# VectorE's order around the Strassen pairs, the quad weights' loads spread over more places, and four token buffers instead of two

## The chip, the cores and the metric

One core of a Trainium2 chip runs the whole program. The metric is the device time of one execution in microseconds, as the median of several runs. The engines named below are TensorE (PE in the profile, its weight loads PEld), VectorE (DVE), ScalarE (ACT), GpSimd (POOL) and SyncE (SP), which issues almost all DMAs and issues them in order.

## What is computed

An attention block (a gated outer-product recurrence over 768 steps, 4 batches, 8 heads, head size 48) gives a 3072 x 384 matrix. Its rows are then sent to one of eight experts each:

```python
logits = x @ w_gate
expert_idx = np.argmax(logits, axis=1)
...
for e in range(E):
    lo, hi = (boundaries[e], boundaries[e + 1])
    ...
    h = np.maximum(x_sorted[lo:hi] @ w1[e], 0.0)
    y_sorted[lo:hi] = h @ w2[e]
y = y_sorted[inv_perm]
return (gate_w[:, None] * y).astype(np.float32)
```

Here `w1[e]` is 384 x 1024 and `w2[e]` is 1024 x 384, all in float32. The change touches only this second part.

## The kernel before

The first part of the program (attention, routing, and a first tile of 128 rows of experts 0 and 1) is a block of its own, whose instructions stand in an order that is written out by hand. It scatters the rows into the DRAM tensor `xs`, one region to an expert. Its last VectorE steps are `turn(rows_of[0])`, which turns the rows of expert 0 round (written `xT`, L320), and the writing out of the early tile of expert 1.

The second block, again with its order written by hand on every engine, goes over the eight experts. Between the two blocks the framework's scheduler may interleave the two lists of an engine; within a block each engine keeps the order of the code. For each expert `e`:

- `weight_sums` makes three sums of pieces of `w2` on VectorE (`wsum`, L1162, 128x768 each).
- `widen` multiplies the rows with `w1` in eight blocks of 128 hidden columns (TensorE, `hps`, L337). ScalarE and VectorE take turns in moving the results out of PSUM through the ReLU (L347, L349) into `hT`. There are four PSUM banks for this. Experts 0 and 1 have 256 rows left here, two blocks to a bank; experts 2 and 3 have 384 rows, experts 4 to 7 have 352, one block to a bank.
- `hidden_sums` makes two sums of pieces of `hT` on VectorE (`hsum`, L1246, and one at L1162).
- `turn` of the next expert's rows (VectorE, `xT`, one buffer; L320, and `dst`, L326).
- Narrowing. The third tile of experts 2 and 3 is a plain product with `w2` (L353). The third tile of experts 4 to 7 holds 96 rows of the expert and 32 rows of another ("riding", L1143, 128x384). The first two tiles together form one Strassen product, `narrow_pair`: seven products of eight matmuls (L1194), with further sums on VectorE between them (`a[0][0]`, `a[0][1]` of `hT`, and `b[0][1]` of `w2t`, all L1162), ScalarE holding parts (`held`, L1205) and VectorE joining them (`joined`, L1209).

Rows beyond an expert's own room are gathered into two "quads" of four groups of 32 rows, each group with the weights of its own expert (`qw`, eight loads of 1.5 MB to a quad, issued on SP by `fetch` at places numbered 2e and 2e+1: `FIRST_AT` for the first weights, `SECOND_AT` for the second). Quad 0 is widened with expert 4 and quad 1 with expert 7 (`widen_quad`, L1117); `turn_quad` then turns the result with sixteen small VectorE transposes (`hqT`, L1137), four to a group. Quad 0's groups ride with experts 4 to 7, one each; quad 1 is narrowed at the very end (`narrow_quad`, L1143, 128x192).

SP loads, within expert `e`, the rows of expert e+2 (`xrow`, L290, four DMAs), their token numbers and gates (`tg`, L305, two buffers), the first weights of e+2 (L400), the pieces of `fetch(2e)`, the second weights of e+2 (L405), and the pieces of `fetch(2e+1)`. The buffers of a `tg` come free when `narrow_pair` two experts earlier has read its gates.

Of the kernel before, what the change touches and what calls it, by code (L numbers as in the profile page):

```python
# [11 lines left out]
F32 = mybir.dt.float32  # L12
# [8 lines left out]
C = 128  # L21
# [11 lines left out]
E, F = 8, 1024  # L33
NF = F // 128

TILES = 3
# [11 lines left out]
WITH = {4: 0, E - 1: 1}  # L48
# [2 lines left out]
FIXED = np.array([SHORT if e in RIDE else TILES * C for e in range(E)])  # L51

ROWS_AT = {2: 0, 9: 1}
FIRST_AT = {h: (q, g) for q, at in ((0, (3, 4, 5, 6)), (1, (10, 11, 12, 13))) for g, h in enumerate(at)}
SECOND_AT = {3: (0, 0), 4: (0, 1), 5: (0, 2), 6: (0, 3), 10: (1, 0), 11: (1, 1), 13: (1, 2)}

BK = 32
DB = DM // (128 // BK)
# [3 lines left out]
EARLY = 2  # L62

TOK, GATE, USED, ROW = DM, DM + 1, DM + 2, DM + 16
# [57 lines left out]
def kernel(  # L122
# [161 lines left out]
    rowp = ctx.enter_context(tc.tile_pool(name="rowp", bufs=2))  # L284
# [12 lines left out]
    def load_rows(row, count=C):  # L297

        rows = xs[ds(row, count)] if not isinstance(row, int) else xs[row : row + count]
        n, whole = -(-count // C), count // C  # L300
        x = rowp.tile([128, TILES * C // BK, DB], F32, name="xrow")[:, 0 : count // BK]
        tg = rowp.tile([128, TILES, USED - TOK], F32, name="tg")[:, 0:n]
        reads = load_blocks(x, rows)
        reads.append(
            nc.sync.dma_start(  # L305
                tg[:, 0:whole], rows[0 : whole * C, TOK:USED].rearrange("(t p) r -> p t r", p=C)
            ).ins
        )
        if n > whole:
            nc.sync.dma_start(tg[0 : count - whole * C, whole], rows[whole * C :, TOK:USED])  # L310
        return {"n": n, "rows": count, "x": x, "tg": tg, "reads": reads}
# [16 lines left out]
    def widen(x, w, bank, blocks):  # L328

        rows = x["rows"]  # L330
        per = 512 // rows
        for b in blocks:
            i, f = divmod(b, per)
            if f == 0:
                x["h"] = bank(i)[:, 0 : per * rows].rearrange("p (f c) -> p f c", f=per)
            for j in range(KD):
                nc.tensor.matmul(  # L337
                    x["h"][:, f],
                    lhsT=w[0][:, j, b * 128 : b * 128 + 128],
                    rhs=x["xT"][:, j],  # L340
                    start=j == 0,
                    stop=j == KD - 1,
                )
            if f == per - 1:
                to = x["hT"][:, b - f : b + 1]
                if i % 2 == 0:
                    nc.scalar.activation(to, x["h"], AF.Relu)  # L347
                else:
                    nc.vector.tensor_scalar(to, x["h"], 0.0, None, op0=OP.max)  # L349
# [725 lines left out]
    with ExitStack() as st:  # L1075
# [21 lines left out]
        def quad_first(q, g):  # L1097
            x = quads[q]
            if g == 0:
                x["first"] = qp.tile([128, 4, KD, F], F32, name="qw1")  # L1100
            quad_weights(x["first"][:, g], q, g, moe_w1, W1)

        def quad_second(q, g):
            quads[q]["second"][g] = w2 = qp.tile([128, NF, DM], F32, name="qw2", bufs=4)
            quad_weights(w2, q, g, moe_w2, W2)

        def pieces():
            return [(g, slice(g * T, g * T + T)) for g in range(4)]
# [19 lines left out]
                    nc.vector.tensor_scalar(hq[:, b], hp[b], 0.0, None, op0=OP.max)  # L1128
            x["hq"] = hq

        def turn_quad(x):

            x["hT"] = qp.tile([128, NF, C], F32, name="hqT", bufs=2)
            hq = x["hq"].rearrange("p b f (j c) -> p j (b f) c", c=T)
            for g, r in pieces():
                for j, to in pieces():
                    nc.vector.transpose(x["hT"][to, :, r], hq[r, j])  # L1137

# [22 lines left out]
        def minus(to, a, b):  # L1161
            nc.vector.tensor_tensor(to, a, b, op=OP.subtract)  # L1162

        def weight_sums(w):

            b = [
                [w[1][:, HB * i : HB * i + HB, HD * j : HD * j + HD] for j in range(2)]
                for i in range(2)
            ]
            t1, t2, t4 = (qp.tile([128, HB, HD], F32, name=f"wsum{i}") for i in (1, 2, 4))  # L1170
            minus(t1, b[0][1], b[0][0])
            minus(t2, b[1][1], t1)
            minus(t4, b[1][0], t2)
            return b, t1, t2, t4
# [5 lines left out]
                for t in range(2)  # L1180
            ]

        def narrow_pair(x, s1, sums):

            b, t1, t2, t4 = sums
            a = hidden_parts(x)
            one, two, both = (psz.tile([128, DM], F32, name="yps") for i in range(3))
            one, two, left, right = one[:, 0:HD], two[:, 0:HD], both[:, 0:HD], both[:, HD:DM]
            ysb = [ep.tile([128, DM], F32, name="ysb") for t in range(2)]
            gate = [x["tg"][:, t, 1:2] for t in range(2)]  # L1190

            def product(to, h, w, start):
                for f in range(HB):
                    nc.tensor.matmul(  # L1194
                        to,
                        lhsT=h[:, f],
                        rhs=w[:, f],
                        start=start and f == 0,
                        stop=f == HB - 1,
                        skip_group_check=True,  # L1200
                    )

            def held(part, t):
                to = qp.tile([128, HD], F32, name="held", bufs=3)
                nc.scalar.mul(to, part, gate[t])  # L1205
                return to

            def joined(t, h, part, other):
                nc.vector.scalar_tensor_tensor(  # L1209
                    ysb[t][:, h * HD : h * HD + HD],  # L1210
                    part,
                    gate[t],
                    other,
                    op0=OP.mult,
                    op1=OP.add,
                )

            def leave(t):
                scatter(out, x["dst"][:, t : t + 1], ysb[t], N - 1, "out")

            minus(b[0][1], b[1][1], b[0][1])
            product(one, a[0][0], b[0][0], True)
            p1 = held(one, 0)
            minus(a[0][0], s1, a[0][0])
            product(left, a[0][1], b[1][0], True)
            minus(a[0][1], a[0][1], a[0][0])
            product(right, a[1][1], t4, True)
            joined(0, 0, left, p1)
            p4 = held(right, 1)
            product(two, s1, t1, True)  # L1230
            p5 = held(two, 1)
            product(one, a[0][0], t2, False)
            u2 = held(one, 0)
            product(two, a[0][1], b[1][1], False)
            joined(0, 1, two, u2)
            leave(0)
            product(one, a[1][0], b[0][1], False)
            joined(1, 0, one, p4)
            joined(1, 1, one, p5)
            leave(1)  # L1240
# [19 lines left out]
        def fetch(half):  # L1260
            if half in ROWS_AT:
                quads[ROWS_AT[half]] = quad_rows(ROWS_AT[half])
            if half in FIRST_AT:
                quad_first(*FIRST_AT[half])
            if half in SECOND_AT:
                quad_second(*SECOND_AT[half])

        for e in range(E):
            x, w = rows_of[e], weights[e]
            end = e == E - 1  # L1270
            x["hT"] = qp.tile([128, NF, TILES * C], F32, name="hT")[:, :, 0 : x["rows"]]
            sums = weight_sums(w)
            widen(x, w, bank, range(NF))
            if e in WITH:
                widen_quad(quads[WITH[e]])
            s1 = hidden_sums(x)
            if e + 1 < E:
                turn(rows_of[e + 1])
            if e + 1 in WITH:
                turn(quads[WITH[e + 1]], qp)  # L1280
            if e + 2 < E:
                rows_of[e + 2] = load_expert(e + 2)
                load_first_weights(e + 2)
            fetch(2 * e)
            if e in WITH and not end:
                turn_quad(quads[WITH[e]])
            if e in RIDE:
                narrow_riding(x, w, quads[0], RIDE[e])
            if end:
                nc.gpsimd.drain()  # L1290
                quad_second(1, 3)
                halves_of(quads[WITH[e]], 0)
                turn_quad(quads[WITH[e]])
            for t in range(2, TILES - 1 if e in RIDE else x["n"]):
                narrow_late(x, t, w)
            narrow_pair(x, s1, sums)
            if end:
                narrow_quad(quads[WITH[e]])
            if e + 2 < E:
                load_second_weights(e + 2)  # L1300
            fetch(2 * e + 1)
# [156 lines left out]
```

## Time and profile before

| | |
|---|---|
| median of 3 runs | 402.71 us (402.61 to 405.11) |
| profiled execution, its own time | 400.64 us |
| its span | 398.6 us |
| mean granted TensorE clock | 0.976 |
| PEld, busy | 293.8 us (74%) |
| ACT, POOL, busy | 115.1 us (29%), 105.2 us (26%) |
| DMA, mean over the span | 238 GB/s |

The span runs from the first to the last instruction of the program on the core; the execution's own time is 2.04 us longer. Busy shares are means over the whole span, so they don't tell which stage waits for what. In a timeline row stand the start, the duration, the engine, the line, what is written and read, and in square brackets the idle time of the engine before it with what ended that. In a row of waits stand the total, the count and the longest.

### The profile page before, as it was taken

What the parts mean: (1) busy time and instruction counts of PE and PEld (TensorE: products, weight loads), DVE (VectorE), ACT (ScalarE), POOL (GpSimd) and SP (SyncE); (2) the same over time, 40 slices, a digit from 0 to 9 for tenths busy, and PEclk for the clock granted to TensorE, in tenths of its full rate; (3) what the DMA queues carried; (4) which work ended last, traced back from release to release, by engine and by line L of the source; (5) the groups of instructions that cost most, each with busy time, mean ns of one, the idle gap of its engine ahead of it and who ended that gap; (6) DMA issues with size and microseconds to landing.
All of it is one profiled execution on the core that took longest, in us unless ns stands there. A gap on an engine that the chain in (4) does not pass through costs nothing.

```text
span 398.6 us, 8241 instructions
## 1 busy us (share of the span) xinstructions
PE 377.1 (95%) x3246; PEld 293.8 (74%) x3246; DVE 223.3 (56%) x447; ACT 115.1 (29%) x222; POOL 105.2 (26%) x120
## 2 busy tenths in 40 slices
PE   8999999999999969999999999977999999999774
PEld 8889989889997849897568568522964965963573
DVE  6999989897856244636254164137344435422740
ACT  6998867784231001111001001100110110201010
POOL 5453357479746010202012012000210210200002
PEclk9999999999999989999999999996999999999969
DMA  8999766759964559492489999890073389990501
GB/s 272 385 363 373 241 238 217 255 173 371 406 204 161 171 150 310 78 349 53 176 280 299 351 394 321 344 339 14 16 248 123 89 304 384 403 400 20 178 10 55
DMA packets 51663, 94.86 MB, mean 238 GB/s; under 512 B 20840, under 2 KB 40875, under 8 KB 49568
## 3 DMA queue, kind: packets, MB, share of 16 engines
q1 hardware_dynamic: 48448, 84.62, 63.3%
q0 software_dynamic: 3168, 9.64, 6.5%
q8 instruction: 27, 0.44, 0.5%
q14 instruction: 20, 0.16, 0.1%
HBM read 79.23 MB, written 15.21 MB: 237 GB/s over the span
## 4 chain that ended last, share of the span: by engine, by line
PE 79%; DMA 8%; DVE 6%; issue 2%; SPq 2%; ACT 1%; POOL 0%; POOLq 0%; DVEq 0%
PE hps L337 26%; PE yps L1194 15%; PE yps L1143 7%; PE s L594 6%; PE xp L717 6%; PE yt L618 6%; DMA w2t<-in_moe_w_dram 4%; PE yps L353 3%; PE yt L639 3%; PE kp L607 3%; PE dp L655 2%; DVE hqT L1137 2%; DMA fpack<-c_fpack 2%; PE hps L1117 1%; PE s L337 1%
## 5 line engine op out<-in xcount | busy, mean ns | idle before, releaser
L337 PE MATMUL hps<-xT,w1t 128*128 128x352 f32 (+2 forms) x384 | 111.8, 452 | 4.0 <-DVE xT L320 3.4
L337 PEld LDWEIGHTS hps<-xT,w1t 128*128 128x128 f32 x384 | 73.9, 193 | 39.4 <-issue 4.0
L196 POOL DMA_INDIRECT out_dram<-ysb,dst x24 | 29.3, 1223 | 232.2 <-DVE ysb L364 144.7
L349 DVE TENSOR_SCALAR hT<-hps 128x352 f32<-128x352 f32 (+2 forms) x28 | 15.6, 558 | 74.0 <-PE hps L337 74.0
L1194 PE MATMUL yps<-w2t,hT 128*128 128x192 f32 x256 | 46.3, 336 | 0.5 <-ACT held L1205 0.5
L1194 PEld LDWEIGHTS yps<-w2t,hT 128*128 128x128 f32 x256 | 43.5, 196 | 4.2 <-issue 2.5
L347 ACT ACTIVATE hT<-hps 128x352 f32<-128x352 f32 (+2 forms) x28 | 13.7, 490 | 111.3 <-PE hps L337 95.8
L1205 ACT ACTIVATE held<-yps,tg 128x192 f32<-128x192 f32 x32 | 12.9, 420 | 103.3 <-PE yps L1194 55.0
L1143 PE MATMUL yps<-qw,hqT 128*32 128x192 f32 (+1 forms) x192 | 29.7, 397 | 4.7 <-DVE hqT L1137 4.7
L600 DVE COPY_PREDICATED at<-mpack,s 128x512 f32<-128x512 uint8 x48 | 32.1, 731 | 3.1 <-PE s L594 3.1
L1209 DVE SCALAR_TENSOR_TENSOR ysb<-yps,tg,held 128x192 f32<-128x192 f32 x32 | 12.6, 415 | 37.1 <-PE yps L1194 37.1
L560 POOL TENSOR_TENSOR k<-k,r 128x1024 f32<-128x1024 f32 (+1 forms) x11 | 25.2, 2294 | 20.5 <-ACT r L556 14.6
L1194 PE MATMUL yps<-wsum,hT 128*128 128x192 f32 x128 | 25.0, 341 | 4.6 <-DVE hT L1162 4.6
L542 DVE TENSOR_TENSOR_SCAN sum<-g,cap 128x1032 f32<-128x1032 f32 (+1 forms) x14 | 28.2, 2019 | 2.0 <-ACT g L535 1.9
L196 POOL DMA_INDIRECT xs<-xr,posi x24 | 25.4, 1060 | 13.5 <-issue 4.6
L594 PE MATMUL s<-q,k 64*128 64x128 f32 x384 | 26.3, 282 | 0.1
L1194 PEld LDWEIGHTS yps<-wsum,hT 128*128 128x128 f32 x128 | 22.2, 199 | 5.2 <-issue 5.1
L717 PE MATMUL xp<-wx,ys 128*128 128x104 f32 x192 | 24.9, 279 | 0.2 <-ACT ys L681 0.2
L594 PEld LDWEIGHTS s<-q,k 64*128 64x128 f32 x384 | 22.8, 188 | 2.6 <-issue 1.2
L1143 PE MATMUL yps<-w2t,hT 128*32 128x384 f32 x192 | 24.5, 539 | 0.0
L618 PE MATMUL yt<-at,v 128*48 128x128 f32 x384 | 24.3, 276 | 0.0
L717 PEld LDWEIGHTS xp<-wx,ys 128*128 128x128 f32 x192 | 22.9, 192 | 1.0 <-ACT ys L681 0.3
(130 smaller groups left out, 497.2 us busy)
## 6 DMA issues: line engine op xcount, KB each, us to landing
qw<-in_moe_w_dram SPq DMA_DIRECT2D x16, 1536.0 KB, 15.0
w1t<-in_moe_w_dram SPq DMA_DIRECT2D x8, 1536.0 KB, 8.2
w2t<-in_moe_w_dram SPq DMA_DIRECT2D x8, 1536.0 KB, 15.7
k<-in_ku_dram SPq DMA_DIRECT2D x12, 512.0 KB, 5.3
q<-in_qu_dram SPq DMA_DIRECT2D x12, 512.0 KB, 6.0
f<-in_fu_dram SPq DMA_DIRECT2D x10, 512.0 KB, 6.0
xs<-pad SPq DMA_DIRECT2D x8, 600.0 KB, 4.6
v<-in_vu_dram SPq DMA_DIRECT2D x12, 384.0 KB, 7.0
```

Of the source, the lines that this page charges most:

```text
L196: ins = nc.gpsimd.indirect_dma_start(out=dst, out_offset=bass.IndirectOffsetOnAxis(ap=idx, axis=0), in_=src, in_offset=None, bounds_check= ...
L337: nc.tensor.matmul(x["h"][:, f], lhsT=w[0][:, j, b * 128 : b * 128 + 128], rhs=x["xT"][:, j], start=j == 0, stop=j == KD - 1,)
L347: nc.scalar.activation(to, x["h"], AF.Relu)
L349: nc.vector.tensor_scalar(to, x["h"], 0.0, None, op0=OP.max)
L542: nc.vector.tensor_tensor_scan(x["sum"][:, part].rearrange("p s c -> p (s c)"), x["g"][:, part].rearrange("p s c -> p (s c)"), cap[:, part ...
L560: ins = on.tensor_tensor(k, k, units[u]["r"][:, part], op=OP.mult).ins
L594: done["score"] = nc.tensor.matmul(ps[h][:, p], lhsT=x["k"][r, s], rhs=x["q"][r, s], start=True, stop=True).ins
L600: nc.vector.copy_predicated(x["at"][:, a, h], _bc(causal, 1, HP), x["ps", a][h])
L618: nc.tensor.matmul(x["yt"][a][DP * (h ^ a) : DP * (h ^ a) + D, p], lhsT=x["v"][:, a, 2 * p + h], rhs=x["at"][:, a, h, p], start=p == 0, st ...
L717: nc.tensor.matmul(x["xp", a][:, p], lhsT=x["ys", a][:, p], rhs=wx[:, p, 0:XW] if a else wx[:, p, E:WX], start=True, stop=True,)
L1143: nc.tensor.matmul(yp[r], lhsT=h[:, f, at : at + T], rhs=w[:, f, cols], start=f == 0, stop=f == NF - 1, skip_group_check=True,)
L1194: nc.tensor.matmul(to, lhsT=h[:, f], rhs=w[:, f], start=start and f == 0, stop=f == HB - 1, skip_group_check=True,)
```

## The change

Five things are moved, and one number is set.

1. `weight_sums` stands behind the first four blocks of `widen` instead of ahead of it.
2. In `narrow_pair` the sum `b[0][1]` moves from the front to behind the two sums of `hT`.
3. The turning of the next expert's rows moves, for experts 0 and 1, into `narrow_pair`, behind the first `joined`. For experts 2 to 6 it stays behind `hidden_sums`.
4. Quad 0 is widened between the sixth and seventh block of expert 4. One group (four transposes) is turned right behind it, the other three behind the pair.
5. Quad 1 is still widened behind expert 7, but `hidden_sums` comes ahead of it. Two of its groups are turned ahead of the riding tile and two inside the pair, where all four were turned between the riding tile and the pair.
6. The quads' first weights are fetched at places 2, 3, 4, 5 and 10, 11, 12, 12 (before: 3 to 6 and 10 to 13), the second weights at 6 to 9 and all three at 13 (before: 3 to 6 and 10, 11, 13). `tg` has four buffers.

```diff
-FIRST_AT = {h: (q, g) for q, at in ((0, (3, 4, 5, 6)), (1, (10, 11, 12, 13))) for g, h in enumerate(at)}
-SECOND_AT = {3: (0, 0), 4: (0, 1), 5: (0, 2), 6: (0, 3), 10: (1, 0), 11: (1, 1), 13: (1, 2)}
+FIRST_AT = {2: [(0, 0)], 3: [(0, 1)], 4: [(0, 2)], 5: [(0, 3)], 10: [(1, 0)], 11: [(1, 1)], 12: [(1, 2), (1, 3)]}
+SECOND_AT = {6: [(0, 0)], 7: [(0, 1)], 8: [(0, 2)], 9: [(0, 3)], 13: [(1, 0), (1, 1), (1, 2)]}
...
-        tg = rowp.tile([128, TILES, USED - TOK], F32, name="tg")[:, 0:n]
+        tg = rowp.tile([128, TILES, USED - TOK], F32, name="tg", bufs=4)[:, 0:n]
...
-        def turn_quad(x):
+        def turn_quad(x, some):
...
-            for g, r in pieces():
+            for g, r in pieces()[some]:
                 for j, to in pieces():
                     nc.vector.transpose(x["hT"][to, :, r], hq[r, j])
...
-        def narrow_pair(x, s1, sums):
+        def narrow_pair(x, s1, sums, between=lambda: None):
...
-            minus(b[0][1], b[1][1], b[0][1])
             product(one, a[0][0], b[0][0], True)
             p1 = held(one, 0)
             minus(a[0][0], s1, a[0][0])
             product(left, a[0][1], b[1][0], True)
             minus(a[0][1], a[0][1], a[0][0])
+            minus(b[0][1], b[1][1], b[0][1])
             product(right, a[1][1], t4, True)
             joined(0, 0, left, p1)
+            between()
...
+            quad = quads[WITH[e]] if e in WITH else None
+
+            def turn_next():
+                if e + 1 < E:
+                    turn(rows_of[e + 1])
+                if e + 1 in WITH:
+                    turn(quads[WITH[e + 1]], qp)
+
+            widen(x, w, bank, range(4))
             sums = weight_sums(w)
-            widen(x, w, bank, range(NF))
-            if e in WITH:
-                widen_quad(quads[WITH[e]])
+            if quad and not end:
+                widen(x, w, bank, range(4, 6))
+                widen_quad(quad)
+                turn_quad(quad, slice(0, 1))
+                widen(x, w, bank, range(6, NF))
+            else:
+                widen(x, w, bank, range(4, NF))
             s1 = hidden_sums(x)
-            if e + 1 < E:
-                turn(rows_of[e + 1])
-            if e + 1 in WITH:
-                turn(quads[WITH[e + 1]], qp)
+            if end:
+                widen_quad(quad)
+                halves_of(quad, 0)
+                turn_quad(quad, slice(0, 2))
+            elif e >= EARLY:
+                turn_next()
...
-            if e in WITH and not end:
-                turn_quad(quads[WITH[e]])
             if e in RIDE:
                 narrow_riding(x, w, quads[0], RIDE[e])
             if end:
                 nc.gpsimd.drain()
                 quad_second(1, 3)
-                halves_of(quads[WITH[e]], 0)
-                turn_quad(quads[WITH[e]])
             for t in range(2, TILES - 1 if e in RIDE else x["n"]):
                 narrow_late(x, t, w)
-            narrow_pair(x, s1, sums)
             if end:
-                narrow_quad(quads[WITH[e]])
+                narrow_pair(x, s1, sums, lambda: turn_quad(quad, slice(2, 4)))
+                narrow_quad(quad)
+            else:
+                narrow_pair(x, s1, sums, turn_next if e < EARLY else lambda: None)
+                if quad:
+                    turn_quad(quad, slice(1, 4))
```

More of the change, by code (lines that the diff above doesn't have):

```diff
@@ L1129, in widen_quad @@
             x["hq"] = hq
-        def turn_quad(x):
-            x["hT"] = qp.tile([128, NF, C], F32, name="hqT", bufs=2)
+        def turn_quad(x, some):
+            if "hT" not in x:
+                x["hT"] = qp.tile([128, NF, C], F32, name="hqT", bufs=2)
             hq = x["hq"].rearrange("p b f (j c) -> p j (b f) c", c=T)
-            for g, r in pieces():
+            for g, r in pieces()[some]:
                 for j, to in pieces():
@@ L1262, in fetch @@
                 quads[ROWS_AT[half]] = quad_rows(ROWS_AT[half])
[L1263 to L1266, printed above, removed]
+            for piece in FIRST_AT.get(half, ()):
+                quad_first(*piece)
+            for piece in SECOND_AT.get(half, ()):
+                quad_second(*piece)
         for e in range(E):
```

## The prediction, written before the changed kernel ran

> **What bounds the kernel now.** I read the page's shares first, then TensorE's own waits, then the chain that ended last, and last the timeline around each wait.
>
> ```profile
> span 398.6 us, 8241 instructions
> ...
> PE 377.1 (95%) x3246; PEld 293.8 (74%) x3246; DVE 223.3 (56%) x447; ACT 115.1 (29%) x222; POOL 105.2 (26%) x120
> ...
> PE yps L1143 <- DVE hqT L1137: 4.7, 1, 4.7
> PE yps L1194 <- DVE hT L1162: 4.6, 2, 4.2
> PE hps L337 <- DVE xT L320: 3.4, 1, 3.4
> PE hps L337 <- ACT hT L347: 0.6, 1, 0.6
> ```
>
> TensorE is the bound: 95% busy. VectorE is at 56% and yet ends all its long waits, three of them, once each. So VectorE isn't short of time. It is late in three places. They show in the timeline:
>
> ```profile
> 134.78 5.41 PE L353 MATMUL yp<-w2t,hT 128*128 128x384 f32 x16
> 136.30 0.14 DVE L1047 CAST fixi<-fix 1x1 int32<-1x1 f32 x1
> 140.38 0.96 DVE L1162 TENSOR_TENSOR wsum<-w2t 128x768 f32<-128x768 f32 x1 [3.94 <-PE yp L353]
> 142.25 1.20 DVE L320 STREAM_TRANSPOSE xT<-xrow 128x768 f32<-128x768 f32 x1
> 143.59 8.62 PE L337 MATMUL hps<-xT,w1t 128*128 128x256 f32 x31 [3.40 <-DVE xT L320]
> ...
> 267.98 1.58 DVE L320 STREAM_TRANSPOSE xT<-xrow 128x1056 f32<-128x1056 f32 x1
> 269.51 7.19 DVE L1137 STREAM_TRANSPOSE hqT<-hq 32x256 f32<-32x256 f32 x16
> 271.34 0.85 PE L1143 MATMUL yps<-qw,hqT 128*32 128x384 f32 x1 [4.72 <-DVE hqT L1137]
> ...
> 371.85 7.17 DVE L1137 STREAM_TRANSPOSE hqT<-hq 32x256 f32<-32x256 f32 x16
> 379.04 0.96 DVE L1162 TENSOR_TENSOR w2t<-w2t 128x768 f32<-128x768 f32 x1
> 380.74 2.90 PE L1194 MATMUL yps<-wsum,hT 128*128 128x192 f32 x8 [4.22 <-DVE hT L1162]
> ```
>
> At 140 the turning of expert 0's rows stands behind two weight sums, which stand behind TensorE's last early tile. At 271 the riding tile waits for the turning of quad 0, behind `xT`. At 381 the Strassen pair waits for its sums, behind sixteen transposes and `b[0][1]`. A gap costs more than its length, as the granted clock (before the DMA share and GB/s at the end of the row) shows:
>
> ```profile
> 140.00:150.00 10.00, 6.59 (x23) 5.35 (x23) 4.46 (x6) 0.60 (x1) 1.44 (x1) 0.83 0.53 156
> 270.00:280.00 10.00, 8.66 (x61) 3.03 (x62) 6.86 (x16) 0.00 (x0) 0.00 (x0) 0.66 0.01 3
> 380.00:390.00 10.00, 9.26 (x84) 8.61 (x88) 2.78 (x6) 1.15 (x3) 1.94 (x2) 0.68 0.07 23
> ```
>
> So I price whole stages by the chain, a disturbed stage against an undisturbed one of the same work:
>
> ```profile
> 143.59 12.30 PE hps L337 x48
> 165.59 10.37 PE hps L337 x48
> 186.19 15.48 PE hps L337 x48
> 206.83 9.10 PE yps L1194 x56
> ...
> 245.67 6.65 PE hps L337 x23
> 288.89 14.20 PE hps L337 x48
> ...
> 308.39 9.30 PE yps L1194 x56
> 317.69 14.20 PE hps L337 x48
> ...
> 346.48 14.20 PE hps L337 x48
> 360.68 5.29 PE hps L1117 x48
> 365.97 5.20 PE yps L1143 x64
> ...
> 387.69 5.38 PE yps L1143 x128
> ```
>
> **The change part by part.** *Weight sums behind four blocks.* In the second block's list VectorE's first instruction is now an eviction of expert 0, which needs `xT`. The sums can't slip ahead of `turn` any more. The turn itself needs its rows:
>
> ```profile
> 131.42 2.18 SPq L290 DMA_DIRECT2D xrow<-xs  x4
> xrow<-xs SPq DMA_DIRECT2D x4, 96.0 KB, 3.0
> ```
>
> They are issued by 133.60 and land 3.0 us later, at 136.6; VectorE is free at 136.44. So `xT` is done at about 137.9, and TensorE goes on at 134.78 + 5.41 = 140.19 without a stop. The stage took 143.59 + 12.30 - 140.19 = 15.70 us. The same 48 matmuls take 10.37 for expert 1. **Gain 5.33.** The sums cost 2.9 us (three of 0.96) behind the evictions of blocks 1 and 3. With 352 rows a block takes 14.20/8 = 1.78: block 3's eviction ends at 7.7 into the stage, the sums at 10.6, and block 5's is due at 10.7. Nothing waits. If the sums were late, three further banks cover some 3.5 us.
>
> *Expert 1's and 2's turns inside the pair, `b[0][1]` later.* The pair of expert 0 took 165.59 - 155.89 = 9.70 us and that of expert 1 186.19 - 175.96 = 10.23, against 9.10 undisturbed. The rows of expert 1:
>
> ```profile
> 181.52 1.54 PE L1194 MATMUL yps<-wsum,hT 128*128 128x192 f32 x8 [0.37 <-DVE hT L1162]
> 183.32 2.87 PE L1194 MATMUL yps<-w2t,hT 128*128 128x192 f32 x16 [0.26 <-ACT held L1205]
> ```
>
> Turn and `b[0][1]` stand ahead of the sum and of the first `joined` that these two wait for; with both out of the way the waits go. **Gain 0.60 + 1.13 = 1.73.** The turn then ends some 6.7 us into the pair, 2.4 ahead of the next `widen`. For experts 2 to 6 `b[0][1]` now delays `joined` by about 0.2 us. ScalarE follows, and TensorE needs its result over a microsecond later: nothing.
>
> *Quad 0 inside expert 4.* From 245.67 to 288.89 the expert took 43.22 us. Expert 5 took 317.69 - 288.89 = 28.80 for the same without a quad, and the quad's matmuls take 5.29 at full clock: 34.09. **Gain 9.13**: the wait of 4.72, the wait of 0.6 for ScalarE's eviction (it stands in this expert, and may return when the banks fall otherwise), and the rest, 3.8, is half clock. Four transposes of 0.45 take 1.8 us while TensorE does two blocks (3.55). The other twelve take 5.4 at the start of expert 5, behind two `joined` of 0.42, so up to 6.2. The first eviction there is due at 3.6 and ends below 7. Its bank is wanted by block 5 at 8.9, so 2 us are left. Beyond that each late microsecond costs one.
>
> *Quad 1 around the last pair.* From 346.48 to 387.69 expert 7 took 41.21 against the same 34.09. **Gain 7.12.** New deadlines, from the start R of the pair:
>
> ```profile
> 312.58 0.42 DVE L1209 SCALAR_TENSOR_TENSOR ysb<-yps,tg,held 128x192 f32<-128x192 f32 x1 [0.66 <-PE yps L1194]
> ...
> 378.00:379.00 1.00, 0.00 (x0) 0.00 (x0) 0.97 (x3) 0.00 (x0) 0.00 (x0) 1.00 0.02 10
> ```
>
> The riding tile starts 5.2 ahead of R, when the quad is done. With 1 us at most for the quad's eviction and two tiny instructions, the first eight transposes run from R - 4.2 to R - 0.6. The first `joined` of expert 6's pair ended at 313.00 with R at 308.39, so at R + 4.6; with `b[0][1]` ahead of it I take R + 4.8. The last eight end at R + 8.4, and `narrow_quad` reads them at R + 9.3: 0.9 us are left. It also reads the last `qw` load, which is issued when the riding tile ends (today at 371.17). In the slice from 378 to 379 the DMAs move almost nothing more (10 GB/s), so it lands by R + 7.8. Today the late pair hides it; then 1.5 us are left. The 5.38 us of `narrow_quad` and the tail behind it stay.
>
> *Loads and four token buffers.*
>
> ```profile
> SPq L305 <- DVE ysb L1209: 59.1, 6, 25.2
> ...
> w2t<-in_moe_w_dram SPq DMA_DIRECT2D x8, 1536.0 KB, 15.7
> ```
>
> SP stood 59.1 us at `tg` until an older pair had read its gates, with the first weights of the next experts queued behind. That goes, but TensorE waits for no DMA in the rows above: gain 0. What is late next on SP are w1's and w2's own buffers, free at the end of `widen` and of the pair; a w2 lands 15.7 us after its issue (median), with a whole expert (28.80) until it is read. Place 2 puts one `qw` ahead of expert 3's w2, and places 7 and 9 put second weights ahead of the rows of experts 6 and 7. Each delays those by its own 1.5 MB, and both are read an expert later. I bound this part by -0.5 and +1.
>
> The sum is 5.33 + 1.73 + 9.13 + 7.12 = 23.31. With half of the 0.6 left standing it is 23.0. The profiled execution (400.64, 398.6 of it span) would fall to 377.6, its span to 375.6. The median of the runs is 2.07 higher, so the forecast is 402.71 - 23.0 = 379.7, 5.7% faster.
>
> [...]
>
> **The rivals.** *Expert 0 starts late all the same* (`xT` waits for something the trace hides behind the sums, or the scheduler puts other work ahead): 5.3 us are not won, 385.0. For it: only the end of a longer wait is seen. Against: rows landed and VectorE idle for 3.94. *The end stalls in a new place:* the last transposes or the last load come after R + 9.3. At 2 to 4 us late with some half clock this gives back 3 to 6: 383 to 386. For it: margins of 0.9 and 1.5 us only. Against: both margins come from rows. *Slower:* TensorE reaches its weights sooner, the loads don't shorten, and a w2 that hasn't landed stops VectorE at `weight_sums` with two evictions behind them, so `widen` stops once four banks are full. It decides from a landing some 11 us into a stage, and to reach 407 it would have to hold TensorE 27 us in all, say 7 in each of experts 2 to 5. Against: the sums stood up to 8 us earlier in the stage before and waited for no DMA. *No effect:* quad and pair wait for other causes; 402 to 403. Against: the releasers are named in the rows.
>
> **How the numbers follow.** The forecast with all four terms has 0.72, expert 0 late 0.10, the end stalled 0.11, no effect 0.04, slower 0.03. The likeliest case spans 377.0 (0.3 and 0.5 from the terms above, and runs some 2 lower, as the profiled one was) to 382. The range goes to 386 and leaves out 2 in 10 at most. About 1% is what a measurement of this kernel can tell from no change. Faster by over 1%: 0.93; within: 0.04; slower: 0.03.
>
> **What would show it.** TensorE's waits for `xT`, `hqT` and `hT` should be gone or below 0.5 us each; the granted clock should be 1.00 in all slices of the second block; expert 0's 48 matmuls should take 10.4 us straight behind the early tile; expert 4 and expert 7 should take 34.1 each up to the end of the pair; SP's wait for `ysb` at L305 should be gone. It would be wrong if a wait of over 3 us on TensorE stands anywhere behind 140 us.

## The result, and the profile after

| | before | after |
|---|---|---|
| median of 4 runs each, taken together | 402.77 us (402.61 to 405.11) | 381.17 us (380.78 to 381.63) |
| profiled execution, its own time | 400.64 us | 381.11 us |
| its span | 398.6 us | 379.1 us |
| mean granted TensorE clock | 0.976 | 0.995 |

The ratio is 0.9451, with an interval from 0.9415 to 0.9487: 5.5% faster. The forecast was 379.7 us. Ratios here and below are taken over the single runs and not from the two medians (381.17/402.77 is 0.946), and they leave out one run of 386.78 us, of the kernel called loads_back below, which lay 1.5% above that kernel's fastest.

The page of the changed kernel, its shares and the granted clock in forty slices (in tenths, 9 is 90% or more):

```profile
span 379.1 us, 8261 instructions
...
PE 369.5 (97%) x3246; PEld 289.5 (76%) x3246; DVE 224.4 (59%) x447; ACT 115.6 (30%) x222; POOL 99.7 (26%) x120
...
PEclk9999999999999999999999999999999999999998
```

The work is the same: TensorE has 3246 matmuls before and after, VectorE 447 instructions. TensorE is busy 7.6 us less (377.1 to 369.5), although it computes the same products. The granted clock accounts for it. In the kernel before it stood at 0.50 in three stretches behind 140 us: 144.11 to 147.52, 270.40 to 277.23 and 379.63 to 386.46. TensorE was busy for 15.0 of these 17.1 us. At the full clock that work is estimated at half the time, so 7.5 us less. In the changed kernel the clock falls only at 375.45, behind the last matmul. The rest of the 19.5 us by which the span is shorter is idle time.

TensorE's waits in the changed kernel (total, count, longest):

```profile
PE yt L754 <- DVE yt L482: 1.6, 1, 1.6
PE yp L353 <- issue: 0.5, 1, 0.5
...
PE yps L1144 <- issue: 0.4, 2, 0.2
```

The first two lie in the first block, which the change leaves alone. The four long or named waits of before (4.7 for `hqT`, 4.6 for `hT`, 3.4 for `xT`, 0.6 for ScalarE's `hT`) are all gone. A new one is in the last line: two stops of 0.18 us for which no other engine is named.

The chain that ended last, in order of time (start, length, engine, line, number of instructions):

```profile
137.13 5.27 PE yp L353 x16
142.40 10.36 PE hps L337 x48
152.76 9.10 PE yps L1195 x56
...
172.22 9.10 PE yps L1195 x56
...
240.80 10.65 PE hps L337 x36
251.45 5.29 PE hps L1117 x48
256.73 3.75 PE hps L337 x12
260.48 5.30 PE yps L1144 x64
265.78 9.30 PE yps L1195 x56
...
332.67 14.20 PE hps L337 x48
...
357.31 9.30 PE yps L1195 x56
366.61 3.42 PE yps L1144 x80
```

From the early tile to the last quad it is TensorE throughout, one stage straight behind the other. Beside before, stage by stage (us):

| stage | before | forecast | after |
|---|---|---|---|
| end of the early tile | 140.19 | 140.19 | 142.40 |
| from there to the end of expert 0's 48 matmuls | 15.70 | 10.37 | 10.36 |
| pair of expert 0, of expert 1 | 9.70, 10.23 | 9.10, 9.10 | 9.10, 9.10 |
| expert 4 to the end of its pair | 43.22 | 34.09 | 34.28 |
| expert 7 to the end of its pair | 41.21 | 34.09 | 33.94 |
| `narrow_quad` | 5.38 | 5.38 | 6.94 |

Each after-value is the difference of two starts in the chain (expert 4: 275.08 - 240.80, where 275.08 = 265.78 + 9.30; `narrow_quad`: 366.61 to 373.55, where VectorE's last eviction is released; TensorE's own rows end at 373.05).

VectorE in the same execution (a timeline row: start, length, engine, line, what is written and read, count, idle time before):

```profile
139.32 1.23 DVE L320 STREAM_TRANSPOSE xT<-xrow 128x768 f32<-128x768 f32 x1 [0.67 <-DMA xrow<-xs]
...
148.38 0.95 DVE L1163 TENSOR_TENSOR wsum<-w2t 128x768 f32<-128x768 f32 x1
...
275.89 5.39 DVE L1138 STREAM_TRANSPOSE hqT<-hq 32x256 f32<-32x256 f32 x12
281.31 0.52 DVE L349 TENSOR_SCALAR hT<-hps 128x352 f32<-128x352 f32 x1
...
353.02 3.58 DVE L1138 STREAM_TRANSPOSE hqT<-hq 32x256 f32<-32x256 f32 x8
...
362.07 3.61 DVE L1138 STREAM_TRANSPOSE hqT<-hq 32x256 f32<-32x256 f32 x8
```

`xT` now starts when its rows land and is done 1.85 us ahead of the end of the early tile (139.32 + 1.23 = 140.55 against 142.40). The first sum runs 6 us into the stage. The twelve transposes of quad 0 hold expert 5's first VectorE eviction until 6.2 us into its stage (281.31 - 275.08), and TensorE doesn't feel it (14.20 us for that stage's 48 matmuls, as for experts 6 and 7). The last eight transposes end at 365.68, 0.86 us ahead of the first matmul of `narrow_quad` that the timeline shows (366.54).

SP's waits that matter:

```profile
SPq L1095 <- PE yps L1144: 28.6, 1, 28.6
SPq L405 <- PE yps L1195: 21.7, 5, 4.9
...
SPq L305 <- ACT held L1206: 1.6, 1, 1.6
```

The 59.1 us at L305 for `ysb` are gone. SP now stands at L405 until an older `w2` has been read (here by TensorE, and 19.4 us more until VectorE's sums have read it), which the prediction named as next; L1095, where it waits for a `qw` buffer, stood at 28.1 us before.

### The profile page after: what moved, and what is told of

Same layout as the page of the kernel before. It is cut to its first block, busy times and chain, and to the rows that moved or that the text cites. A ratio compares the mean times of both kernels' runs of the same rounds, so it can differ in the third digit from the quotient of the medians.

```text
span 379.1 us, 8261 instructions
## 1 busy us (share of the span) xinstructions
PE 369.5 (97%) x3246; PEld 289.5 (76%) x3246; DVE 224.4 (59%) x447; ACT 115.6 (30%) x222; POOL 99.7 (26%) x120
## 4 chain that ended last, share of the span: by engine, by line
PE 93%; DVE 3%; DMA 2%; SPq 1%; issue 0%; POOL 0%; POOLq 0%
PE hps L337 29%; PE yps L1195 19%; PE yps L1144 7%; PE s L594 6%; PE yt L618 6%; PE xp L717 6%; PE s L337 3%; PE hps L1117 3%; PE yps L353 3%; PE kp L607 3%; PE yt L639 2%; PE dp L655 2%; PE yp L353 2%; DMA fpack<-c_fpack 2%; DVE sum L542 1%; SPq L517 1%
## 5 line engine op out<-in xcount | busy, mean ns | idle before, releaser
L337 PE MATMUL hps<-xT,w1t 128*128 128x352 f32 (+2 forms) x384 | 110.1, 446 | 0.0
L337 PEld LDWEIGHTS hps<-xT,w1t 128*128 128x128 f32 x384 | 72.7, 190 | 34.9 <-issue 0.8
L196 POOL DMA_INDIRECT out_dram<-ysb,dst x24 | 23.3, 972 | 215.8 <-DVE ysb L364 134.5
L1195 PE MATMUL yps<-w2t,hT 128*128 128x192 f32 x256 | 44.6, 328 | 0.0
L1195 PEld LDWEIGHTS yps<-w2t,hT 128*128 128x128 f32 x256 | 41.9, 190 | 3.1 <-issue 2.5
L196 POOL DMA_INDIRECT xs<-xr,posi x24 | 27.2, 1135 | 16.2 <-issue 4.9
L1144 PE MATMUL yps<-qw,hqT 128*32 128x192 f32 (+1 forms) x192 | 27.5, 381 | 0.4 <-issue 0.4
L1195 PE MATMUL yps<-wsum,hT 128*128 128x192 f32 x128 | 23.4, 326 | 0.0
L618 PEld LDWEIGHTS yt<-at,v 128*48 128x48 f32 x384 | 20.3, 123 | 2.4 <-issue 1.3
L1144 PE MATMUL yps<-w2t,hT 128*32 128x384 f32 x192 | 21.4, 487 | 0.0
```

Of the source, the lines that this page charges most:

```text
L196: ins = nc.gpsimd.indirect_dma_start(out=dst, out_offset=bass.IndirectOffsetOnAxis(ap=idx, axis=0), in_=src, in_offset=None, bounds_check= ...
L337: nc.tensor.matmul(x["h"][:, f], lhsT=w[0][:, j, b * 128 : b * 128 + 128], rhs=x["xT"][:, j], start=j == 0, stop=j == KD - 1,)
L618: nc.tensor.matmul(x["yt"][a][DP * (h ^ a) : DP * (h ^ a) + D, p], lhsT=x["v"][:, a, 2 * p + h], rhs=x["at"][:, a, h, p], start=p == 0, st ...
L1144: nc.tensor.matmul(yp[r], lhsT=h[:, f, at : at + T], rhs=w[:, f, cols], start=f == 0, stop=f == NF - 1, skip_group_check=True,)
L1195: nc.tensor.matmul(to, lhsT=h[:, f], rhs=w[:, f], start=start and f == 0, stop=f == HB - 1, skip_group_check=True,)
```

## The experiments

Behind L1117 the line numbers of the changed kernel are one or two higher than before's. Executions differ in where the early tile ends, in both kernels, so each part is compared from that end to the end of the span ("second block"). The unchanged changed kernel took 236.73, 236.16 and 235.10 us there in three profiles, the kernel before 258.44 and 256.63. The runs fall into three sessions, on different chips; medians are compared within a session only.

| run | median us | ratio to before, interval | end of early tile | second block |
|---|---|---|---|---|
| after_again | 382.99 | 0.9471 (0.9387 to 0.9555) | 144.85 | 236.16 |
| before_again | 402.52 (one run) | | 143.87 | 256.63 |
| sums_first | 388.88 | 0.9603 (0.9519 to 0.9687) | 145.49 | 242.2 |
| quad0_back | 389.99 | 0.9649 (0.9562 to 0.9736) | 143.37 | 244.3 |
| quad1_back | 384.09 | 0.9596 (0.9556 to 0.9635) | 140.12 | 240.3 |
| quad1_three | 381.18 | 0.9523 (0.9492 to 0.9554) | 140.32 | 238.4 |
| pair_back | 380.22 | 0.9487 (0.9454 to 0.9520) | 141.29 | 236.9 |
| loads_back | 383.35 | 0.9535 (0.9490 to 0.9580) | 141.19 | 240.2 |
| after_third | 378.08 | 0.9452 (0.9409 to 0.9495) | 140.95 | 235.10 |
| tg_back | 377.93 | 0.9462 (0.9403 to 0.9521) | 140.64 | 235.2 |
| places_back | 378.23 | 0.9457 (0.9399 to 0.9514) | 140.83 | 235.3 |
| quad_whole | 377.45 | 0.9450 (0.9394 to 0.9507) | 140.14 | 235.6 |

First session: up to quad0_back, before 403.31. Second: quad1_back to loads_back, before 401.11, without a run of the unchanged new order. Third: the rest, before 399.53.

### Both kernels again

No edit.

> The changed kernel as it is, a second time. Its first profile began the second block 2.2 us later than the profile of before (142.40 against 140.19 us) and took 1.56 us longer for the last quad (6.94 against 5.38). Theory A, both are chance of one execution: this profile begins the block near 140.2 and takes 5.4 for the quad. Theory B, both belong to the changed program: 142.4 and 6.9 again, span 379 us.

> The kernel before, a second time. Its first profiled execution was 2.07 us under the median of its runs. If the slower runs lose that in the first block, the early tile of expert 1 ends here near 142.3 us instead of 140.19, the second block takes the same as before, and the span is near 400.6. If they lose it in the second block, the tile ends near 140.2 and a wait of the second block is longer.

The gain stands: 382.99 against 403.31. Both kernels end the early tile later than in the first profiles (144.85 and 143.87), so that end moves with the execution or the chip and not with the change. The last quad was slow again in after_again (6.46 us) and not in before_again (5.41), so neither theory of the first expectation held as it stood; after_third below has both near their old values. In after_again the late end came from a wait of the early tile itself (TensorE's timeline, then two windows with the columns of the prediction: start and end, length, TensorE's busy time, and the granted clock third from the end):

```profile
126.98 7.12 PE L353 MATMUL yp<-w2t,hT 128*128 128x384 f32 x16 [2.02 <-ACT hT L347]
```

```profile
124.07:127.48 3.41, 1.39 (x10) 1.06 (x10) 0.80 (x5) 0.60 (x1) 1.21 (x3) 1.00 0.31 120
127.48:130.89 3.41, 3.41 (x7) 1.85 (x6) 3.17 (x14) 0.00 (x0) 1.71 (x2) 0.50 0.13 53
```

A wait of 2.02 us was followed by 3.41 us at half clock (0.50), by estimate 1.7 us lost beside the wait. The kernel before shows the opposite case. In before_again its wait for `xT` was again 3.40 us, and the clock stayed full:

```profile
147.27 10.60 PE L337 MATMUL hps<-xT,w1t 128*128 128x256 f32 x48 [3.40 <-DVE xT L320]
```

```profile
142.28:145.69 3.41, 1.59 (x5) 0.58 (x4) 1.59 (x2) 0.00 (x0) 0.00 (x0) 1.00 0.50 115
145.69:149.10 3.41, 1.83 (x9) 1.65 (x10) 2.87 (x5) 0.00 (x0) 1.13 (x1) 1.00 0.05 3
149.10:152.52 3.42, 3.42 (x17) 3.02 (x16) 0.00 (x0) 0.60 (x1) 0.30 (x1) 1.00 0.78 266
```

The 48 matmuls took 10.60 us there (to 157.87) where they took 12.30 in the chain of the first profile. That is nearly all of the 1.81 us between the two second blocks of the kernel before (258.44 and 256.63). The first profile of the kernel before, whose clock did fall, cut the same way:

```profile
140.70:144.11 3.41, 0.52 (x3) 0.49 (x4) 3.38 (x6) 0.00 (x0) 0.00 (x0) 1.00 0.23 48
144.11:147.52 3.41, 3.41 (x10) 2.66 (x9) 0.77 (x1) 0.00 (x0) 1.44 (x1) 0.50 0.44 138
```

The windows here are as long as this stretch at half clock, 3.41 us.

### The weight sums first

```diff
+            sums = weight_sums(w)
             widen(x, w, bank, range(4))
-            sums = weight_sums(w)
```

> The changed kernel with the weight sums ahead of all eight blocks again. Theory of the prediction: two sums of expert 0 slip ahead of the turning of its rows, TensorE waits about 3.4 us for xT and then runs for a window at half clock, together +5.3 us: about 386.5. Rival: the place of the sums inside the stages matters, or the turning waits for its rows anyway: no wait for xT here, within 1 us of the changed kernel.

VectorE's timeline at the boundary of the two blocks:

```profile
145.68 0.96 DVE L1163 TENSOR_TENSOR wsum<-w2t 128x768 f32<-128x768 f32 x1 [3.94 <-PE yp L353]
146.68 0.96 DVE L1163 TENSOR_TENSOR wsum<-w2t,wsum 128x768 f32<-128x768 f32 x1
147.55 1.19 DVE L320 STREAM_TRANSPOSE xT<-xrow 128x768 f32<-128x768 f32 x1
```

The old picture is back: the second block's sums stand ahead of the first block's `xT`, VectorE idles 3.94 us until the early tile is through with TensorE, and TensorE then waits 3.4 us for `xT`. The clock dips after it (0.83 over the 10 us from 148). The chain:

```profile
148.89 12.03 PE hps L337 x48
160.92 9.10 PE yps L1195 x56
```

From the end of the early tile the stage takes 160.92 - 145.49 = 15.43 us, against 10.36: 5.07 more. A wait of 0.58 us for ScalarE's `hT` also comes back, now in expert 3, and with it 0.84 us. The median is 5.9 us above that of after_again (388.88 - 382.99). So the first step holds, with its size.

### Quad 0 behind all blocks again

```diff
-            if quad and not end:
-                widen(x, w, bank, range(4, 6))
+            widen(x, w, bank, range(4, NF))
+            if quad and not end:
                 widen_quad(quad)
-                turn_quad(quad, slice(0, 1))
-                widen(x, w, bank, range(6, NF))
-            else:
-                widen(x, w, bank, range(4, NF))
...
+            if quad and not end:
+                turn_quad(quad, slice(0, 4))
             if e in RIDE:
...
-                if quad:
-                    turn_quad(quad, slice(1, 4))
```

> The changed kernel with quad 0 widened behind expert 4 and all sixteen of its transposes ahead of the riding tile again. Theory: TensorE waits 4 to 5 us for hqT and then runs 5 to 6 us at half clock, +8.5 to +9.1: about 390. Rival: with the loads earlier and the sums elsewhere the transposes start sooner and the wait is under 3 us with no clock lost: +3 at most.

TensorE's waits, and the window behind the wait:

```profile
PE yps L1144 <- DVE hqT L1138: 4.7, 1, 4.7
```

```profile
265.00:275.00 10.00, 8.38 (x59) 2.75 (x60) 6.89 (x17) 0.00 (x0) 0.00 (x0) 0.66 0.07 24
```

Expert 4 takes 42.35 us (241.77 to 284.12 in the chain) against 34.28: 8.07 more, of which 4.7 is the wait and about 3.4 the clock (10 us at 0.66); 8.5 to 9.1 was expected. The median is 7.0 above after_again. In the kernel before the same stretch took 43.22, so 0.87 more: the wait of 0.6 for ScalarE, which the early sums cause and which isn't here, and 0.27 for which no row names a cause (before_again took 43.01, so part of it is chance).

### Quad 1's turning: all of it late, or three quarters of it

quad1_back:

```diff
-            s1 = hidden_sums(x)
             if end:
                 widen_quad(quad)
-                halves_of(quad, 0)
-                turn_quad(quad, slice(0, 2))
+            s1 = hidden_sums(x)
...
                 quad_second(1, 3)
+                halves_of(quad, 0)
+                turn_quad(quad, slice(0, 4))
...
-                narrow_pair(x, s1, sums, lambda: turn_quad(quad, slice(2, 4)))
+                narrow_pair(x, s1, sums)
```

> The changed kernel with quad 1 as before: widened ahead of the hidden sums, all sixteen transposes between the riding tile and the pair. b[0][1] stays late, so the pair's wait for its sums should be 4.2 - 0.9 = 3.3 us, with 1.7 to 3 us of half clock behind it: +5 to +6.5 for the stage from expert 7's start to the end of the pair. The last quad takes 5.4 us if its slower run in the changed kernel (6.4, with a stop 3.6 us in) comes from TensorE arriving without a pause, and 6.4 if that belongs to the quad itself. [...]

quad1_three keeps the order of `hidden_sums` and turns one group early and three late:

```diff
-                turn_quad(quad, slice(0, 2))
+                turn_quad(quad, slice(0, 1))
...
                 quad_second(1, 3)
+                turn_quad(quad, slice(1, 4))
...
-                narrow_pair(x, s1, sums, lambda: turn_quad(quad, slice(2, 4)))
+                narrow_pair(x, s1, sums)
```

> The changed kernel with one group of quad 1 turned ahead of the riding tile and three (5.4 us) between it and the pair. The wait for the pair's sums should be about 1.6 us. [...] If every wait costs clock in proportion, +2.5 to +3.

TensorE's waits in quad1_back:

```profile
PE yps L1195 <- DVE hT L1163: 3.4, 1, 3.4
...
PE yps L1195 <- ACT held L1206: 1.1, 1, 1.1
```

and in quad1_three, where the wait for `held` is again 1.1:

```profile
PE yps L1195 <- DVE hT L1163: 1.6, 1, 1.6
```

Four transposes fewer in the way (1.8 us) make the wait 1.8 us shorter; the two kernels also differ in where `hidden_sums` stands, which was not varied alone. From the pair's first matmul to its end it takes 14.36 and 12.57 us against 9.37 (357.24 to 366.61 in the changed kernel), so +4.99 and +3.2. The wait of 1.1 us is new to both: `b[0][1]` now stands behind the two sums, so that late sums make the first `joined` late, and ScalarE's `held` after it. The clock stayed at 1.00 behind both waits in the profiled executions (363 to 373 us in quad1_back, 362 to 372 in quad1_three). So the +5 expected of quad1_back came, but not for the reason expected: 3.4 and 1.1 us are waits, for the last 0.5 no row names a cause, and none is half clock. In quad1_three a wait of about 1.6 us was expected, and +2.5 to +3 if every wait cost clock in proportion. The wait came with 1.6 us and no half clock, so the rest of the +3.2 isn't clock; the second wait of 1.1 us was not foreseen either. quad1_back's windows around its two waits:

```profile
358.54:361.95 3.41, 1.89 (x12) 1.60 (x10) 3.31 (x8) 0.00 (x0) 0.00 (x0) 1.00 0.91 336
361.95:365.37 3.42, 1.54 (x8) 1.27 (x8) 3.26 (x7) 0.00 (x0) 0.00 (x0) 1.00 0.01 2
365.37:368.78 3.41, 2.32 (x14) 2.32 (x15) 0.56 (x2) 1.04 (x3) 0.00 (x0) 1.00 0.03 7
```

The wait of 3.36 us, from 360.44 to 363.80, lies across two of these windows. TensorE was busy for 1.89 and 1.54 us of them, and the clock stood at 1.00 in all three. The other executions show a lower clock: 382.96 us at a mean granted clock of 0.991, 385.21 and 385.45 at 0.987, beside 382.37 at 0.998 for the profiled one. They are one kernel with the same order, some 3 us apart. Only one of the four was profiled, so where the others lost clock isn't shown, and 0.991 went with only 0.6 us. The last quad took 5.38 us in quad1_back, but also in quad1_three, pair_back and loads_back, which ran on the same chip, so that part of the expectation decides nothing.

### The pair's order again

```diff
+            minus(b[0][1], b[1][1], b[0][1])
             product(one, a[0][0], b[0][0], True)
...
-            minus(b[0][1], b[1][1], b[0][1])
             product(right, a[1][1], t4, True)
...
-            elif e >= EARLY:
+            else:
                 turn_next()
...
-                narrow_pair(x, s1, sums, turn_next if e < EARLY else lambda: None)
+                narrow_pair(x, s1, sums, lambda: None)
```

> The changed kernel with b[0][1] at the front of the pair and the turning of experts 1 and 2 ahead of the pair again. Theory: the pairs of expert 0 and 1 take 9.7 and 10.2 us instead of 9.1, +1.7 in all, no other stage changes; the last pair is late by nothing. Rival: with VectorE less loaded elsewhere the pairs stay at 9.1 and nothing changes.

The chain, with the three `widen` stages around the two pairs:

```profile
141.29 10.37 PE hps L337 x48
...
161.38 10.37 PE hps L337 x48
...
181.98 15.48 PE hps L337 x48
```

The pairs fill what lies between: 161.38 - 151.66 = 9.72 and 181.98 - 171.75 = 10.23, so 1.75 us more than two times 9.10. Of these, 0.9 stand in the rows of TensorE's waits (0.4 for VectorE's sum, 0.5 for ScalarE's `held`); for the rest no row names a cause. The turning and `b[0][1]` were put back together, so their shares aren't known. This is the smallest step, and the one that came out to 0.02 us (1.73).

### Loads and token buffers

loads_back takes the old places and two buffers, tg_back only the buffers, places_back only the places:

```diff
-FIRST_AT = {2: [(0, 0)], 3: [(0, 1)], 4: [(0, 2)], 5: [(0, 3)], 10: [(1, 0)], 11: [(1, 1)], 12: [(1, 2), (1, 3)]}
-SECOND_AT = {6: [(0, 0)], 7: [(0, 1)], 8: [(0, 2)], 9: [(0, 3)], 13: [(1, 0), (1, 1), (1, 2)]}
+FIRST_AT = {3: [(0, 0)], 4: [(0, 1)], 5: [(0, 2)], 6: [(0, 3)], 10: [(1, 0)], 11: [(1, 1)], 12: [(1, 2)], 13: [(1, 3)]}
+SECOND_AT = {3: [(0, 0)], 4: [(0, 1)], 5: [(0, 2)], 6: [(0, 3)], 10: [(1, 0)], 11: [(1, 1)], 13: [(1, 2)]}
...
-        tg = rowp.tile([128, TILES, USED - TOK], F32, name="tg", bufs=4)[:, 0:n]
+        tg = rowp.tile([128, TILES, USED - TOK], F32, name="tg")[:, 0:n]
```

> The changed kernel with two token buffers and the old places of the quads' loads. Prediction: no stage of TensorE waits for a DMA either way, 0 within 1 us, SP's long waits for ysb at the tg loads return. Rival: widening quad 0 earlier in expert 4 needs its first weights earlier; with the old places the last one (place 6, issued behind expert 3's first weights) lands after 251 us and TensorE waits there, or the rows and weights behind a blocked tg come late: a wait of 1 us or more on qw, w1t or xT.

> The changed kernel a third time, as the reference for the three kernels beside it. If the two short stops in the last quad (6.4 instead of 5.4 us) and the late early tile (142.4 to 144.9 us instead of 140) go with the chip and not with the program, both are here or absent in all four kernels alike.

> The changed kernel with two token buffers, the new places of the quads' loads kept. In the run with both put back TensorE waited 2.35 us for qw in quad 0's widening. If the places carry that, there is no wait for a DMA here and the time is that of the changed kernel within 1 us, though SP waits for ysb at the tg loads again (about 50 us). If the buffers carry it, the wait for qw is here, +3 to +5 us.

> The changed kernel with the old places of the quads' loads, four token buffers kept. If the places carry the wait for qw (place 6 stands behind expert 3's tg, rows and first weights, issued when expert 3 is widened), it is here: 2 us or more in quad 0's widening. If the two buffers alone did it by holding SP, there is no wait: within 1 us of the changed kernel.

With both back the rival of the first expectation came. TensorE waits for a DMA for the first time in any of these profiles behind 140 us (its timeline, then a window):

```profile
253.59 7.03 PE L1117 MATMUL hps<-qw,qxT 128*32 128x512 f32 x42 [2.35 <-DMA qw<-in_moe_w_dram]
```

```profile
250.00:260.00 10.00, 7.65 (x48) 1.90 (x48) 0.63 (x2) 0.60 (x1) 0.00 (x0) 0.83 1.03 383
```

and the chain goes through that load, from its issue to its landing 8.9 us later:

```profile
244.62 8.93 DMA qw<-in_moe_w_dram
```

Quad 0's 48 matmuls take 10.45 us (250.17 to 260.62) instead of 5.3, so 5.1 us more: 2.35 of wait, 1.7 of clock (10 us at 0.83) and 1.1 for which no row names a cause. The second block is 5.1 longer than that of after_third (240.2 against 235.1). With either alone back there is no wait, and the times are those of after_third (377.93 and 378.23 against 378.08). The last first weight of quad 0 is then issued at 215.5 (tg_back) and 231.6 (places_back) and not at 244.6. In tg_back SP waits at L305 almost as long as in the kernel before, and it costs nothing:

```profile
SPq L305 <- DVE ysb L1210: 49.6, 5, 16.3
```

So the long wait of SP is harmless by itself here, and the new places are needed only together with two buffers. What makes either needed is, by the rows, another part of the change: quad 0 is widened two blocks earlier in expert 4. In loads_back the load landed at 253.55; behind all eight blocks the quad would have begun at 239.59 + 14.20 = 253.79 (an estimate; no run had the old loads with the quad behind). After_third is the base of this set. The early tile ends between 140.14 and 140.95 us in all four kernels of its session, and the last quad takes 5.4 us in all four, so both late parts go with the chip or the session and not with the program alone.

### The last quad in one go

```diff
-            for h in range(2):
-                yp = psz.tile([128, DM], F32, name="yps")[:, 0:HD]
-                narrow_pieces(parts, yp, slice(h * HD, h * HD + HD))
-                put_half(x, 0, h, yp, "out", qp)
+            yp = psz.tile([128, DM], F32, name="yps")
+            narrow_pieces(parts, yp)
+            put(x, 0, yp, "out")
```

> The changed kernel with the last quad narrowed in one go of 384 columns instead of two halves of 192, so with half as many matmuls and weight loads, and one output of 196 KB. If the short stops in the last quad come from the supply of instructions, they are gone here and TensorE takes 5.3 us; the tail grows by 0.2 (eviction) and some 0.3 (output): about 0.5 slower than a run without stops, 0.5 faster than one with them. If they stay, they come from something else in that stretch.

This was meant for the stops in the last quad. TensorE's timeline in the first profile of the changed kernel:

```profile
366.54 3.49 PE L1144 MATMUL yps<-qw,hqT 128*32 128x192 f32 x80
370.21 0.55 PE L1144 MATMUL yps<-qw,hqT 128*32 128x192 f32 x6 [0.18 <-issue]
370.94 2.11 PE L1144 MATMUL yps<-qw,hqT 128*32 128x192 f32 x42 [0.18 <-issue]
```

and in after_third, the same program on another chip:

```profile
365.09 5.41 PE L1144 MATMUL yps<-qw,hqT 128*32 128x192 f32 x128
```

On this chip there was nothing to win: 5.37 us in one go beside 5.41, a tail that is half a microsecond longer (0.2 of it the one wide eviction, 0.63 against 0.43), and medians of 377.45 and 378.08 whose intervals overlap. As a test of the stops it decides nothing.

## Why the prediction was right

**The mechanism and the sum.** Each of the four terms came out within 0.2 us of its stage (table above): 15.70 - 10.36 = 5.34 for expert 0, 0.60 + 1.13 for the pairs, 43.22 - 34.28 = 8.94 for quad 0, 41.21 - 33.94 = 7.27 for quad 1; together 23.28, where 23.31 was forecast. The second block as a whole fell by 258.44 - 235.10 = 23.34 in after_third, which ran on another chip, and by 258.44 - 236.73 = 21.71 in the first profile, which lost 1.56 us in the last quad. In the one session that profiled both kernels it fell by 256.63 - 236.16 = 20.47: before_again had 1.7 us less of half clock, and after_again lost 1.1 in the last quad. So the full 23.3 is the sum under the clock of the first profile. Each step, put back alone, brought its wait back with VectorE as the releaser (for the pairs also ScalarE, which follows it), so the causes are shown and not only the sum. Put back alone they cost 5.1 (and 0.8 in expert 3), 1.75, 8.1 and 5.0. That is 20.7, and 2.3 of the missing 2.6 are quad 1's (7.27 against 4.99): its wait met a half clock in the kernel before and none in quad1_back's profile.

**The hedge of 0.3.** Half of the wait of 0.6 was left standing, since it might return elsewhere. It is absent in every profile with the sums late and moved to expert 3 with the sums first. So it belongs to the sums' place, and the whole 0.6 was won.

**The deadlines.** The last transposes were to end at R + 8.4 with 0.9 us left: they ended at 365.68 = R + 8.4, with 0.86 left. The last `qw` load moved its last bytes by 364.4, R + 7.1, where R + 7.8 was forecast. The rival "the end stalled" didn't come, and no run made `narrow_quad` itself late, so its price of 3 to 6 us is untested. The nearest is quad1_three, whose stall at the start of the pair cost 3.2 us.

**Where the 1.5 us went.** The forecast for the profiled span was 375.6; it was 379.1. Of these 3.5 us, 2.21 are the later end of the early tile (142.40 against 140.19), which the change doesn't touch and which moves by 4 us among executions of either kernel; 1.56 are lost in the last quad; the rest of the second block was 0.27 better. Against the median only about the last quad's part is left (381.17 - 379.7 = 1.5), since the forecast had put back the 2.07 us by which the profiled execution was early. "The 5.38 us of `narrow_quad` and the tail behind it stay" is the statement that failed there and in the first session, and held in the two later ones.

**What the profile was taken from.** Before's own profile held a half clock behind the `xT` wait that before_again, with the same wait, didn't have: 1.7 of the 5.33 us were chance. The falls of the medians (21.6, 20.3 and 21.45 us) lie below 23.3 in all sessions that have both kernels; that fits, but the clock of the unprofiled runs is known only as a mean.

**"Loads: gain 0" was true and incomplete.** Against the kernel before, the loads alone would have brought nothing by the rows, as TensorE waited for no DMA; that was not run. But the prediction set them at zero without asking what the other parts do to their deadline. Moving quad 0 forward by two blocks used up the slack of its first weights, and without the loads' part the kernel was 5.1 us longer (loads_back), outside the bounds of -0.5 and +1 that stood there. The step that has to be added to that term is: who reads this load earlier now?

**The clock.** The forecast priced the waits by what their stages had lost, clock included. For the waits of 4.2 to 4.7 us the rows bear that out: the 10-us windows behind them stand at 0.66 and 0.68 in the kernel before and at 0.66 in quad0_back, so 3.2 to 3.4 us of full clock are missing in each. For shorter waits the cost differed from one execution to the next. The 10-us windows with the waits of 2.02 us (after_again), 2.35 (loads_back) and 3.40 (before) stand at 0.83, so 1.7 us are missing in each, while waits of 3.40 us (before_again) and 3.36 (quad1_back) left the clock at 1.00. So in these runs the length of a wait did not settle by itself what it cost in clock.

## What to carry to other kernels

An engine that is busy 56% of the time can still end every long wait on the one that is the bound. Look for the few places where it is late, price each as a disturbed stage against an undisturbed twin, and move what isn't due yet behind what is. Two parts that look independent may share a margin: check each transfer's deadline against the new order, and undo the parts together as well as alone before calling one useless. A span from a single profile carries chance of some microseconds here, in the clock behind a wait and in parts that nobody touched, so compare stages before spans.

## What the hardware showed that was not expected

- **The same wait cost clock in one execution and none in another.** In the kernel before, TensorE's wait of 3.40 us for `xT` was followed by 3.41 us at a granted clock of 0.50 (144.11 to 147.52), and the 48 matmuls took 12.30 us. In before_again the same wait of 3.40 us left the clock at 1.00, and they took 10.60: 1.7 us in one and nothing in the other. A wait of 3.36 us left it at 1.00 too (quad1_back), and a shorter one of 2.02 us was followed by 3.41 us at 0.50 (after_again). With the waits of 4.72 and 4.22 us in the kernel before it stood at 0.50 for 6.83 us each time (270.40 to 277.23 and 379.63 to 386.46). What else than the length of a wait decides is not shown by these runs.
- **Stops with no releaser in the last quad.** In four profiles of the new order or a variant of it, in the first runs and the first session, its 128 matmuls took 6.43 to 6.94 us with one or two stops between the 66th and the 86th. The named stops are 0.2 to 0.4 us in all, so most of the 1.0 to 1.6 us lost stands in no row of waits. Both profiles of the kernel before in those same sessions took 5.4 us, as did all eight in the later sessions, the unchanged new order among them (quad_whole with 64 matmuls of twice the width). It is neither the program alone nor shown to be the chip alone, and its cause is open.
- **The scheduler's freedom at a block boundary cost 5 us.** Each block keeps its written order, and yet the second block's first VectorE instructions went ahead of the first block's last in both profiles of the kernel before and in sums_first, and not when the second block began with an eviction that needs what the first block makes. In sums_first the stage took 15.43 us against 10.36.
